# Attention's products in four visits for five, with the value sums in one gap

## The chip, the core and the metric

The kernel runs on one core of a Trainium2 chip. A core has TensorE for matmuls (PE in the profile; PEld is its weight load), VectorE (DVE), ScalarE (ACT), GpSimd (POOL) and SyncE (SP), which issues most of the transfers. Each engine works through its own instructions in order and waits on semaphores that the others raise. Matmuls write to PSUM, which has eight banks of 512 fp32 columns. The metric is the device time of one execution in microseconds.

## The reference

Four layers on x of 2048 tokens by 512 features, in the order A, B, A, B, each x + layer(layernorm(x)). There are 32 heads of 16 features. A is a linear attention with learned features and is not touched by the change. B cuts the tokens into four segments of 512. For each segment and head it computes

```python
logits = jnp.einsum("bhqd,bhkd->bhqk", qs, ks) * scale + mask   # causal, 512 x 512
p = _softmax(logits, axis=-1)
a_dot = jnp.einsum("bhqk,bhkd->bhqd", p, vs)
num = jnp.einsum("bhld,bhde->bhle", pq, M)                      # memory of earlier segments
den = jnp.einsum("bhld,bhd->bhl", pq, z)[..., None] + 1e-6
o = g * (num / den) + (1.0 - g) * a_dot
M = M + jnp.einsum("bhld,bhle->bhde", pk, vs)                   # pk = phi(ks)
z = z + jnp.einsum("bhld->bhd", pk)
```

and then o @ wo. Everything is fp32 in and out.

## The kernel before

A layer B is `LayerB.steps`. Four segments times four chunks of eight heads times two make 32 half chunks of four heads, numbered m = 0 to 31. The four heads of a half chunk are two for each half of the PE array: e = 0 uses rows 0 to 63, e = 1 rows 64 to 127, and r = 0, 1 counts the heads in each half. [...] The 512 queries and keys of a head are four blocks of 128.

Work comes in three kinds. `maxima` multiplies queries by keys into the banks mx (e = 0) and my (e = 1), and VectorE takes the row maximum of each product with the causal mask added (`tensor_tensor_reduce`, in the profile CUSTOM_DVE_ANT_0 and a read of the accumulator). `put_maxima` turns the sixteen columns of maxima with a transpose and sends them back, by a transfer from ScalarE's queue, as one more row of the queries, so that the logits come out reduced by their maximum. `attend` multiplies keys by queries (transposed logits) into lg, a tile of two banks, ScalarE takes the Exp into an SBUF tile of tag P4, and GpSimd sets the part above the diagonal to zero (`affine_select`). `weighted` multiplies these by the values, 16 matmuls on four column strips of the array, into the bank pv; ScalarE copies pv to U, and `finish` transposes U and lets VectorE divide by the sums (`weigh`), whose result GpSimd adds to the memory's part.

Time in `steps` is counted in gaps k, R = 5 to a half chunk. At the start of each gap stands a visit: one round of `attend` for the half chunk at hand (`next(at)`) and one of `maxima` for a later one (`next(ma)`, LEAD = 9 gaps ahead). The five rounds of `attend` are block 0 of r = 0, block 0 of r = 1, blocks 1 and 3 of r = 0, the same of r = 1, and block 2 of both. After the visit come steps that were put off (`late`: names that end in ~ in the tables, mostly VectorE's low part of a product that was split into a rounded high part and the rest), then, in gaps 0 and 2, half of `weighted` for the half chunk before, then `later` (the feature map of a projection, on ScalarE and GpSimd), and then what the tables FIRST, GAPS, LAST or FINAL list for that gap, such as a projection in quarters (q, k, v, out), `fin` for `finish`, `a` for the memory's product and its weighing, `t` and `m` for the update of the memory, `turn` for transposed rows, `ln` or `n` for a step of the layer norm. In gaps 0 and 2 the tables list nothing of size.

All of these, but for visits and value sums, take their PSUM tile from the tag g with G = 3 banks. So the eight banks are 3 g, 2 lg, mx, my, pv. Which of the three a tile gets is decided when the program is built; a matmul that opens a tile waits for the last reader of the bank's previous tile. VectorE's, ScalarE's and GpSimd's instructions keep the order in which they are written (`Ordered`), PE's too (`held`).

Layer A's second pass runs as side work in the first gaps of a layer B, and the next layer A's first pass in its last.

## Time and profile before

| | us |
|---|---|
| median of 3 runs | 1522.89 (1522.32 to 1524.72) |
| the profiled execution's own time | 1523.71 |
| its span, first to last instruction | 1521.9 |
| first layer B's half chunks | from 320.6 to about 768 |
| second layer B's half chunks | from 1064.9 to 1504 |

The profile was taken on one execution. A row of the timeline gives the start in us from the start of the span, the duration, the engine, the line, the operation, what it writes and reads (out<-in by tile names), the shape and how many such instructions follow one another; in brackets stands idle time before it and what ended it. Almost all rows have lines L163, L185 or L189, which are helpers, so tiles tell more than lines. A matmul's row is longer than the time to the next matmul's start, because matmuls overlap; the time between starts is what counts on PE.

### The profile page before, as it was taken

The page shows a single profiled execution, that of the slowest core. Times are in us where ns is not written, and L with a number is a line of the kernel's source. Part 1 is how long each engine was busy: PE and PEld are TensorE (multiplying, and loading weights), DVE is VectorE, ACT ScalarE, POOL GpSimd, SP SyncE. Part 2 cuts the span into 40 slices and gives each one's busy share as a digit, 9 for nine tenths or more (in the row PEclk, how much of TensorE's full clock was granted, in tenths as well). Part 3 has the DMA queues.
Part 4 walks back from the last instruction along what each step waited for, and adds up shares of the span by engine and source line. Part 5 has one row for each costly group of instructions (what it writes and reads, how often), then busy time and mean ns, then how long its engine had stood idle before and what let it go on. Part 6 is the DMA issues. An engine that isn't in the chain of part 4 may idle for free.

```text
span 1521.9 us, 30316 instructions
## 1 busy us (share of the span) xinstructions
PE 1456.3 (96%) x10888; PEld 1033.4 (68%) x10888; DVE 1095.3 (72%) x3258; ACT 787.1 (52%) x1178; POOL 650.3 (43%) x1000
## 2 busy tenths in 40 slices
PE   7999989999999999999999998999999999999998
PEld 6877767765666666666667786776656666666554
DVE  4765868668778877878656667757688788787783
ACT  5554335436565566556544333443565656655553
POOL 1668654313454544433314445541344445444331
PEclk9999999999999999999999999999999999999999
DMA  5487265545444443535340122744463353443340
GB/s 183 129 289 254 70 210 165 167 119 153 122 110 117 135 104 103 157 99 147 114 143 33 39 84 80 225 148 144 113 175 106 105 153 99 111 118 98 80 112 36
DMA packets 108773, 195.85 MB, mean 129 GB/s; under 512 B 14416, under 2 KB 27856, under 8 KB 107856
## 3 DMA queue, kind: packets, MB, share of 16 engines
q1 hardware_dynamic: 107472, 193.38, 42.8%
q8 instruction: 88, 1.44, 0.4%
q10 hardware_dynamic: 1152, 0.52, 0.1%
q14 instruction: 61, 0.50, 0.1%
HBM read 101.05 MB, written 39.85 MB: 93 GB/s over the span
## 4 chain that ended last, share of the span: by engine, by line
PE 78%; DVE 12%; ACT 4%; issue 2%; POOL 2%; DMA 1%; SPq 0%; ACTq 0%; POOLq 0%; DVEq 0%
PE g L185 45%; PE pv L185 9%; PE lg L185 9%; PE g L189 7%; PE mx L185 5%; PE my L185 3%; DVE mx L163 2%; POOL P L163 2%; DVE es L163 2%; ACT P L163 1%; DVE my L163 1%; DVE mxs L163 1%; ACT tb L163 1%; DVE hl L163 1%; DVE ol L163 1%
## 5 line engine op out<-in xcount | busy, mean ns | idle before, releaser
L163 ACT ACTIVATE P<-lg 128x1024 f32<-128x1024 f32 x320 | 328.9, 1028 | 173.0 <-PE lg L185 165.5
L163 POOL TENSOR_SCALAR_AFFINE_SELECT P<-P 128x256 f32<-128x256 f32 (+1 forms) x448 | 190.7, 440 | 442.3 <-ACT P L163 441.7
L163 DVE CUSTOM_DVE_ANT_0 mx<-mx,mask 128x128 f32<-128x128 f32 (+3 forms) x512 | 255.3, 499 | 160.7 <-PE my L185 109.0
L163 DVE CUSTOM_DVE_ANT_0 my<-my,mask 128x128 f32<-128x128 f32 (+3 forms) x512 | 265.9, 519 | 6.5
L185 PE MATMUL g<-hh,wqk 128*128 128x512 f32 x512 | 180.5, 407 | 2.1 <-ACT hh L163 1.4
L185 PE MATMUL lg<-e,e 64*128 64x256 f32 (+2 forms) x1024 | 168.4, 387 | 7.8 <-ACT P L163 7.6
L185 PE MATMUL g<-w,oh 128*128 128x512 f32 x512 | 170.6, 414 | 3.5 <-DVE ol L163 1.6
L185 PE MATMUL pv<-P,v 128*32 128x512 f32 (+3 forms) x2048 | 165.0, 441 | 0.0
L185 PE MATMUL my<-e,e 63*128 63x256 f32 (+2 forms) x512 | 146.7, 346 | 5.3 <-DVE mxs L163 3.9
L185 PEld LDWEIGHTS lg<-e,e 64*128 64x128 f32 x1024 | 81.1, 184 | 103.2 <-issue 50.6
L185 PE MATMUL g<-w,hh 128*128 128x512 f32 x448 | 145.8, 406 | 0.9 <-ACT tb L163 0.9
L163 DVE DVE_READ_ACCUMULATOR2_ANT mxs<- 128x1 f32 x1024 | 145.0, 142 | 0.0
L185 PE MATMUL mx<-e,e 63*128 63x256 f32 (+2 forms) x512 | 140.8, 330 | 0.2
L185 PEld LDWEIGHTS pv<-P,v 128*32 128x32 f32 x2048 | 53.7, 109 | 100.9 <-issue 92.0
L185 PEld LDWEIGHTS g<-hh,wqk 128*128 128x128 f32 x512 | 96.3, 188 | 24.0 <-ACT hh L163 1.8
L185 PEld LDWEIGHTS g<-w,oh 128*128 128x128 f32 x512 | 89.4, 190 | 30.9 <-issue 5.7
L185 PE MATMUL g<-w,ol 128*128 128x512 f32 x256 | 101.8, 398 | 0.0
L185 PE MATMUL g<-hl,wqk 128*128 128x512 f32 x256 | 100.4, 392 | 0.4 <-DVE hl L163 0.4
L163 POOL TENSOR_SCALAR tb<-tb 128x512 f32<-128x512 f32 x48 | 71.5, 1489 | 67.4 <-ACT tb L163 67.4
L163 ACT CAST ta<-g 128x512 fp32r<-128x512 f32 x64 | 37.6, 587 | 112.5 <-PE g L185 112.2
L185 PEld LDWEIGHTS my<-e,e 63*128 63x128 f32 x512 | 82.0, 185 | 18.1 <-DVE mxs L163 8.8
L185 PEld LDWEIGHTS mx<-e,e 63*128 63x128 f32 x512 | 89.7, 186 | 6.1 <-issue 3.6
(143 smaller groups left out, 2816.8 us busy)
## 6 DMA issues: line engine op xcount, KB each, us to landing
e<-ta SPq DMA_DIRECT2D x384, 128.0 KB
wqk<-wqk SPq DMA_DIRECT2D x64, 512.0 KB
x<-x SPq DMA_DIRECT2D x48, 256.0 KB
ot<-in SPq DMA_DIRECT2D x28, 256.0 KB
pq<-tb SPq DMA_DIRECT2D x24, 256.0 KB
tb<-pq SPq DMA_DIRECT2D x24, 256.0 KB
x<-xr SPq DMA_DIRECT2D x24, 256.0 KB
xr<-x SPq DMA_DIRECT2D x24, 256.0 KB
```

The source lines that it names most:

```text
L163: i = f(*a, **k)
L185: return held(nc.tensor.matmul(*a, **k))
L189: return held(nc.tensor.transpose(*a))
```

## The change

R goes from 5 to 4. `attend` has four rounds, one for each r and e: block 0 of one head of half e and blocks 1 and 3 of the head of the other half, in lg, then one Exp and two masks. The rounds with r = 1 have block 2 of both heads of half e too, in a bank of its own, mz, with an Exp of 512 columns and one mask. `maxima` also has four rounds; the first and the last hold two more products each, in mz. `attend` uses mz in gaps 2 and 3 and `maxima` in gaps 0 and 1. `weighted` runs once, in gap 0, with all 16 products; its tile comes from g, and the bank pv is gone (8 banks: 3 g, 2 lg, mx, my, mz). The tables are written anew for four gaps: what stood in gap 3 stands in gap 2, and what stood in gap 4 in gap 3; LEAD, FINAT, BEGIN, MAXIMA and BEFORE follow. The diff, cut (FIRST, LAST, FINAL and BEFORE change in the same manner as GAPS):

```diff
-PV = 1
 G = 3
-R = 5
-FILL = (1, 3, 4)
-LEAD = 9
-FINAT = 8
+R = 4
+LEAD = 7
+FINAT = 6
...
-BEGIN = -25
-MAXIMA = -9
+BEGIN = -22
+MAXIMA = -7
...
 GAPS = """
-0.2 n              | 0.3 a1 fin v3/3 n
-0.1 max a1 k2~     | 0.4 v3 turn~ m0
-1.0 n              | 1.2 n
-1.1 max q3~        | 1.3 fin out/2     | 1.4 out t1 turn~
-2.1 max a2 m1 k3~  | 2.3 fin ln out/3  | 2.4 out turn~ ln
-3.1 max ln ln out~ | 3.3 a2 fin q0+/2  | 3.4 q0+~ t2
-4.1 max k0+~ a3 turn~ load | 4.3 a3 fin out/3 | 4.4 out~ m2
-5.0 n              | 5.3 fin v0+/2 n N
-5.1 max q1+~ begin | 5.4 v0+ t3
-6.0 N              | 6.1 max a0+ k1+~  | 6.2 n
-6.3 a0+ fin v1+/3 N | 6.4 v1+ m3       | 7.0 n N
-7.1 max q2+~       | 7.2 n N           | 7.3 fin v2+/2 n N
-7.4 v2+ t0+
+0.2 a1 fin v3/3 n
+0.1 max a1 k2~ n   | 0.3 v3 turn~ m0
+1.0 n
+1.1 max q3~ n      | 1.2 fin out/2     | 1.3 out t1 turn~
+2.1 max a2 m1 k3~  | 2.2 fin ln out/3  | 2.3 out turn~ ln
+3.1 max ln ln out~ | 3.2 a2 fin q0+/2  | 3.3 q0+~ t2
+4.1 max k0+~ a3 turn~ load | 4.2 a3 fin out/3 | 4.3 out~ m2
+5.0 n              | 5.2 fin v0+/2 n N
+5.1 max q1+~ begin | 5.3 v0+ t3
+6.0 N              | 6.1 max a0+ k1+~ n
+6.2 a0+ fin v1+/3 N | 6.3 v1+ m3       | 7.0 n N
+7.1 max q2+~ n N   | 7.2 fin v2+/2 n N
+7.3 v2+ t0+
 """
...
-            for what in ([(0, 0, 0), (0, 2, P)], [(0, 3, 0)], [(1, 0, 0), (1, 2, P)],
-                         [(0, 1, 0), (1, 1, 256)], [(1, 3, 0)]):
+            for r, e, three in ((0, 1, True), (0, 0, False), (1, 1, False), (1, 0, True)):
                 pb = [PS(t, 1) for t in ("mx", "my")]
-                for r, i, at in what:
-                    prod(pb, r, i, at, max(256, (i + 1) * P))
-                for e in range(2):
-                    for r, i, at in what:
-                        top(pb, e, r, i, at)
+                parts = [(pb[1 - e], 1 - e, r, 0, 0), (pb[1 - e], 1 - e, r, 2, P), (pb[e], e, r, 3, 0)]
+                if three:
+                    pz = PS("mz", 1)
+                    parts.insert(0, (pz, e, 0, 1, 0))
+                    parts.insert(2, (pz, e, 1, 1, 256))
+                for part in parts:
+                    prod(*part)
+                if not three:
+                    parts = [parts[i] for i in (0, 2, 1)]
+                for part in parts:
+                    top(*part)
                 self.mx[m] = mx
                 yield
...
-            for kbs, r in (((0,), 0), ((0,), 1), ((1, 3), 0), ((1, 3), 1), ((2,), None)):
-                pb = PS("lg", 1, (P, 2, 512))
...
+            for r in range(2):
+                for e in range(2):
+                    f = 1 - e
+                    pb = PS("lg", 1, (P, 2, 512))
+                    pr = T2("P4", NP4, shape=(P, 2, 512))
...
+                    prod(pb[:, f, 256:512], f, r, 3, 256)
+                    prod(pb[:, e, :], e, r, 0, 512)
+                    prod(pb[:, f, 0:384], f, r, 1, 384)
+                    exp_of(pr, pb, pr[:, e : e + 1, 0:P], pr.rearrange("p e (b x) -> p e b x", b=4)[:, f, 0:4:3, :])
+                    if r > 0:
+                        pz = PS("mz", 1)
+                        if e == 0:
+                            p2 = T2("P4", NP4, shape=(P, 2, 512))
+                        for rr in range(2):
+                            prod(pz[:, 256 * rr : 256 * rr + 256], e, rr, 2, 256)
+                            self.pr[m][2, rr, e] = p2[:, e, 256 * rr : 256 * rr + 256]
+                        exp_of(p2[:, e, :], pz, p2[:, e, :].rearrange("p (r x) -> p r x", r=2)[:, :, 0:P])
+                    yield
...
-            if not last:
-                self.pv[m] = PS("pv", PV)
-            pv, pr = self.pv[m], self.pr[m]
-            for kb in ((1, 2) if last else (0, 3)):
+            pv, pr = PS("g", G), self.pr.pop(m)
+            for kb in (0, 3, 1, 2):
...
-            for k in range(BEGIN, R * N + 4):
+            for k in range(BEGIN, R * N + 1):
...
-                if k % R in (0, 2) and 0 <= k // R - 1 < N:
-                    self.weighted(k // R - 1, k % R == 2)
+                if k % R == 0 and 0 <= k // R - 1 < N:
+                    self.weighted(k // R - 1)
```

More of the change, by code (lines that the diff above doesn't have):

```diff
@@ L52 @@
 FIRST = """
-0.1 max k2/2       | 0.2 v3/2          | 0.3 k2~
-0.4 v3             | 1.1 max m0 q3/2   | 1.3 fin q3~       | 1.4 t1 k3/1
-2.1 max m1 k3      | 2.3 fin ln~       | 2.4 ln~ ln~
-3.3 fin q0+/2      | 3.0 w
-3.1 max ln~        | 3.4 q0+~ t2
-4.1 max k0+/2 load | 4.3 fin k0+/1     | 4.4 k0+ m2
-5.0 n              | 5.3 fin q1+/2 n
-5.1 max v0+        | 5.4 q1+~ t3
-6.1 max a0+ v1+    | 6.2 n             | 6.3 a0+ fin k1+/2
-6.4 k1+ m3         | 7.0 n             | 7.2 n
-7.1 max q2+~       | 7.3 fin v2+/2 n   | 7.4 v2+ t0+
+0.0 v3/2
@@ L64 @@
+0.1 max k2/2       | 0.2 k2~           | 0.3 v3
+1.1 max m0 q3/2    | 1.2 fin q3~       | 1.3 t1 k3/1
+2.1 max m1 k3      | 2.2 fin ln~       | 2.3 ln~ ln~
+3.2 fin q0+/2      | 3.0 w
+3.1 max ln~        | 3.3 q0+~ t2
+4.1 max k0+/2 load | 4.2 fin k0+/1     | 4.3 k0+ m2
+5.0 n              | 5.2 fin q1+/2 n
+5.1 max v0+        | 5.3 q1+~ t3
+6.1 max a0+ v1+ n  | 6.2 a0+ fin k1+/2
+6.3 k1+ m3         | 7.0 n
+7.1 max q2+~ n     | 7.2 fin v2+/2 n   | 7.3 v2+ t0+
 """
 GAPS = """
-0.2 n              | 0.3 a1 fin v3/3 n
@@ L79 @@
+7.3 v2+ t0+
 """
 LAST = """
-0.1 max a1 k2~     | 0.2 n             | 0.3 a1 fin v3/3 n
-1.0 n              | 0.4 v3 turn~      | 1.2 n
-1.1 max q3~        | 1.3 fin out/2     | 1.4 out turn~
-2.1 max k3~        | 2.3 fin a2 out/2  | 2.4 out a2 turn~
-3.1 max ln~ ln~    | 3.3 fin out/2 ln~ | 3.4 out ln~ turn~
-4.1 max v/2        | 4.3 fin out/2     | 4.4 out v
-5.1 max v/2        | 5.3 fin v         | 5.4 a3 pre
-6.1 max v/2        | 6.3 fin v a3      | 6.4 v/2 pt~
-7.1 p v pt~        | 7.3 fin v/2 p pt  | 7.4 v p pt
+0.1 max a1 k2~ n   | 0.2 a1 fin v3/3 n
@@ L91 @@
+1.0 n              | 0.3 v3 turn~
+1.1 max q3~ n      | 1.2 fin out/2     | 1.3 out turn~
+2.1 max k3~        | 2.2 fin a2 out/2  | 2.3 out a2 turn~
+3.1 max ln~ ln~    | 3.2 fin out/2 ln~ | 3.3 out ln~ turn~
+4.1 max v/2        | 4.2 fin out/2     | 4.3 out v
+5.1 max v/2        | 5.2 fin v         | 5.3 a3 pre
+6.1 max v/2        | 6.2 fin v a3      | 6.3 v/2 pt~
+7.1 p v pt~        | 7.2 fin v/2 p pt  | 7.3 v p pt
 """
 FINAL = """
-0.1 max k2~        | 0.3 fin v3/3      | 0.4 v3 a1
-1.1 max a1 q3/2    | 1.3 fin q3~       | 1.4 turn~
@@ L95 @@
-2.1 max k3/2       | 2.3 fin k3        | 2.4 out/2
-3.1 max a2 out turn~ | 3.3 fin out/2   | 3.4 out~ a2
-4.1 max a3 turn~   | 4.3 fin out/2     | 4.4 out/1 a3
-5.1 max out turn~  | 5.3 fin out/2     | 5.4 out/1 pre
-6.1 max out~       | 6.3 fin           | 6.4 pt~
-7.1 p pt~          | 7.3 fin p pt      | 7.4 p pt
-"""
-BEFORE = {-25: "q0 load", -23: "v0", -21: "k0",
-          -18: "n", -17: "v1 n", -16: "n", -15: "n n", -14: "q1 n", -13: "n", -12: "k1 n", -11: "n", -10: "v2 n",
-          -4: "max q2~", -1: "t0"}
+0.1 max k2~        | 0.2 fin v3/3      | 0.3 v3 a1
@@ new lines @@
+1.1 max a1 q3/2    | 1.2 fin q3~       | 1.3 turn~
+2.1 max k3/2       | 2.2 fin k3        | 2.3 out/2
+3.1 max a2 out turn~ | 3.2 fin out/2   | 3.3 out~ a2
+4.1 max a3 turn~   | 4.2 fin out/2     | 4.3 out/1 a3
+5.1 max out turn~  | 5.2 fin out/2     | 5.3 out/1 pre
+6.1 max out~       | 6.2 fin           | 6.3 pt~
+7.1 p pt~          | 7.2 fin p pt      | 7.3 p pt
+"""
+BEFORE = {-22: "q0 load", -20: "v0", -18: "k0",
+          -15: "n", -14: "v1 n", -13: "n", -12: "n n", -11: "q1 n", -10: "n", -9: "k1 n", -8: "n", -7: "v2 n",
+          -3: "max q2~", -1: "t0"}
@@ L906, in __init__ @@
             self.st, self.hT, self.vv, self.ot, self.mx, self.U = {}, {}, {}, {}, {}, {}
-            self.pr, self.pv = {}, {}
+            self.pr = {}
             self.later, self.late, self.rows, self.turned = [], [], [], []
@@ L1023, in maxima, with prod @@
             mx = T2("mxs", 2, shape=(P, 16))
-            def prod(pb, r, i, at, w):
-                for e in range(2):
-                    q, k = Q[64 * e : 64 * e + 63, r, :], K[64 * e : 64 * e + 63, r, :]
-                    mm(pb[e][:, at : at + w], lhsT=q[:, i * P : (i + 1) * P], rhs=k[:, 0:w],
-                       start=True, stop=True, tile_position=(64 * e, 0))
+            def prod(pb, e, r, i, at):
+                w = max(256, (i + 1) * P)
+                q, k = Q[64 * e : 64 * e + 63, r, :], K[64 * e : 64 * e + 63, r, :]
+                mm(pb[:, at : at + w], lhsT=q[:, i * P : (i + 1) * P], rhs=k[:, 0:w],
+                   start=True, stop=True, tile_position=(64 * e, 0))
             def top(pb, e, r, i, at):
@@ L1033, in top @@
                 col = (e * 2 + r) * 4 + i
-                pl = pb[e][:, at : at + n]
+                pl = pb[:, at : at + n]
                 with tc.high_priority():
@@ L1038, in top @@
                         op0=ADD, op1=MAX, accum_out=mx[:, col : col + 1])
-            for what in ([(0, 0, 0), (0, 2, P)], [(0, 3, 0)], [(1, 0, 0), (1, 2, P)],
-                         [(0, 1, 0), (1, 1, 256)], [(1, 3, 0)]):
+            for r, e, three in ((0, 1, True), (0, 0, False), (1, 1, False), (1, 0, True)):
                 pb = [PS(t, 1) for t in ("mx", "my")]
-                for r, i, at in what:
-                    prod(pb, r, i, at, max(256, (i + 1) * P))
-                for e in range(2):
-                    for r, i, at in what:
-                        top(pb, e, r, i, at)
+                parts = [(pb[1 - e], 1 - e, r, 0, 0), (pb[1 - e], 1 - e, r, 2, P), (pb[e], e, r, 3, 0)]
[9 more added lines that the diff above has]
+                    top(*part)
                 self.mx[m] = mx
@@ L1065, in attend, with prod, exp_of @@
             self.pr[m] = {}
-            def prod(pb, r, kb, at, w):
-                for e in range(2):
-                    q, k = Q[64 * e : 64 * e + 64, r, :], K[64 * e : 64 * e + 64, r, :]
-                    mm(pb[:, e, at : at + w], lhsT=k[:, kb * P : (kb + 1) * P],
-                       rhs=q[:, 512 - w : 512], start=True, stop=True, tile_position=(64 * e, 0))
-            for kbs, r in (((0,), 0), ((0,), 1), ((1, 3), 0), ((1, 3), 1), ((2,), None)):
-                pb = PS("lg", 1, (P, 2, 512))
-                pr = T2("P4", NP4, shape=(P, 2, 512))
-                pq = pr.rearrange("p e (b x) -> p e b x", b=4)
-                if kbs == (0,):
-                    prod(pb, r, 0, 0, 512)
-                    diags = [pr[:, :, 0:P]]
-                elif kbs == (1, 3):
-                    prod(pb, r, 3, 256, 256)
-                    prod(pb, r, 1, 0, 384)
-                    diags = [pq[:, e, 0:4:3, :] for e in range(2)]
-                else:
-                    for rr in range(2):
-                        prod(pb, rr, 2, 256 * rr, 256)
-                    diags = [pr.rearrange("p e (r x) -> p (e r) x", r=2)[:, :, 0:P]]
-                self.pr[m][kbs, r] = pr
+            def prod(out, e, r, kb, w):
+                q, k = Q[64 * e : 64 * e + 64, r, :], K[64 * e : 64 * e + 64, r, :]
+                mm(out, lhsT=k[:, kb * P : (kb + 1) * P],
+                   rhs=q[:, 512 - w : 512], start=True, stop=True, tile_position=(64 * e, 0))
+            def exp_of(pr, pb, *diags):
                 with tc.high_priority():
@@ L1092, in attend, with weighted @@
                     pool.affine_select(out=diag, in_=diag, pattern=[[0, diag.shape[1]], [1, P]],
-                                            compare_op=ALU.is_ge, fill=0.0, base=0, channel_multiplier=-1)
-                yield
-        def weighted(self, m, last):
+                                       compare_op=ALU.is_ge, fill=0.0, base=0, channel_multiplier=-1)
+            for r in range(2):
[3 more added lines that the diff above has]
+                    pr = T2("P4", NP4, shape=(P, 2, 512))
+                    self.pr[m][0, r, e] = pr[:, e, :]
+                    self.pr[m][1, r, f] = pr[:, f, 0:384]
+                    self.pr[m][3, r, f] = pr[:, f, 384:512]
+                    prod(pb[:, f, 256:512], f, r, 3, 256)
[11 more added lines that the diff above has]
+                    yield
+        def weighted(self, m):
             s, c, hf = m // 8, m % 8 // 2, m % 2
             v = self.vv[s][0]
-            if not last:
-                self.pv[m] = PS("pv", PV)
-            pv, pr = self.pv[m], self.pr[m]
-            for kb in ((1, 2) if last else (0, 3)):
+            pv, pr = PS("g", G), self.pr.pop(m)
+            for kb in (0, 3, 1, 2):
                 for r in range(2):
@@ L1107, in weighted @@
                         h = c * 8 + hf * 4 + hh
-                        if kb == 0:
-                            p = pr[(0,), r][:, e, :]
-                        elif kb == 2:
-                            p = pr[(2,), None][:, e, 256 * r : 256 * r + 256]
-                        else:
-                            p = pr[(1, 3), r][:, e, 0:384] if kb == 1 else pr[(1, 3), r][:, e, 384:512]
                         mm(pv[32 * hh : 32 * hh + 32, kb * P : 512],
-                           lhsT=v[:, kb, h * VW : h * VW + 32], rhs=p,
+                           lhsT=v[:, kb, h * VW : h * VW + 32], rhs=pr[kb, r, e],
                            start=(kb == 0), stop=(kb == 2), tile_position=(0, 32 * hh))
-            if last:
-                self.pr.pop(m)
-                U = T2("U", 2)
-                act.activation(U, self.pv.pop(m), AF.Identity, scale=share[:, m % 8 : m % 8 + 1])
-                self.U[m] = U
+            U = self.U[m] = T2("U", 2)
+            act.activation(U, pv, AF.Identity, scale=share[:, m % 8 : m % 8 + 1])
         def finish(self, m):
```

## The prediction

> **What bounds the kernel now.** I read the page first, for the engine that carries the span and for the chain of waits.

> ```profile
> span 1521.9 us, 30316 instructions
> PE 1456.3 (96%) x10888; PEld 1033.4 (68%) x10888; DVE 1095.3 (72%) x3258; ACT 787.1 (52%) x1178; POOL 650.3 (43%) x1000
> PE 78%; DVE 12%; ACT 4%; issue 2%; POOL 2%; DMA 1%; SPq 0%; ACTq 0%; POOLq 0%; DVEq 0%
> ```

> PE is busy for 96% of the span and holds 78% of the chain. Then I cut the two attention stages into stretches (busy time by stretch: PE, PEld, DVE, ACT, POOL); the first row is the second segment of the first layer B, eight half chunks, the second the sum over both stages.

> ```profile
> 429.72:546.87 117.15, 116.57 (x857) 78.58 (x856) 92.24 (x329) 71.07 (x103) 54.74 (x95) 1.00 0.43 119
> sum 874.06, PE 856.92 PEld 560.98 DVE 673.34 ACT 512.16 POOL 366.48; mean PE 107.11 PEld 70.12 DVE 84.17 ACT 64.02 POOL 45.81
> ```

> In the middle segments PE is idle for 0.6 us of 117, and in both stages together for 17 of 874. So whatever the change saves must be saved in PE's own work, and any new wait of PE is added in full. Third, PE's timeline through one half chunk:

> ```profile
> 429.72 0.50 PE L185 MATMUL lg<-e,e 64*128 64x512 f32 x2
> ...
> 430.39 1.28 PE L185 MATMUL pv<-P,v 128*32 128x512 f32 x16
> 431.60 0.50 PE L185 MATMUL lg<-e,e 64*128 64x512 f32 x2
> ...
> 432.44 0.28 PE L189 MATMUL g<-ident,mxs 128*16 128x128 f32 x1
> 432.55 0.63 PE L185 MATMUL g<-mem,tb 128*128 128x136 f32 x4
> ...
> 435.86 0.56 PE L185 MATMUL lg<-e,e 64*128 64x256 f32 x4
> ...
> 436.58 1.28 PE L185 MATMUL pv<-P,v 128*32 128x384 f32 x16
> 437.80 0.56 PE L185 MATMUL lg<-e,e 64*128 64x256 f32 x4
> ...
> 438.64 0.73 PE L185 MATMUL g<-mem,tb 128*128 128x136 f32 x4
> 439.21 0.60 PE L189 MATMUL g<-ident,U 128*128 128x128 f32 x4
> 439.81 0.73 PE L185 MATMUL g<-w,hh 128*128 128x512 f32 x2
> ```

> Each visit starts at an lg row and ends at the next row that is neither lg, mx nor my. The first lasts 0.67 us (512 logit and 512 maxima columns in each half of the array, 1024), the second 0.84 (1152), the third 0.72 (1152), the fourth 0.84 (1280). The fifth has 1024 columns like the first; I take 0.67. Together 3.74 us. Behind the first and the third come the value sums, 1.21 and 1.22 us. Fourth, VectorE's timeline across the third and fourth visits:

> ```profile
> 436.69 0.70 DVE L163 CUSTOM_DVE_ANT_0 mx<-mx,mask 128x512 f32<-128x512 f32 x1 [1.55 <-PE my L185]
> 437.30 0.14 DVE L163 DVE_READ_ACCUMULATOR2_ANT mxs<- 128x1 f32 x1
> ...
> 437.95 0.69 DVE L163 TENSOR_TENSOR ta<-g,ta 128x512 fp32r<-128x512 f32 x1
> 438.68 0.30 DVE L163 CUSTOM_DVE_ANT_0 mx<-mx,mask 128x128 f32<-128x128 f32 x1
> ...
> 439.07 0.57 DVE L163 CUSTOM_DVE_ANT_0 mx<-mx,mask 128x384 f32<-128x384 f32 x1
> 439.55 0.14 DVE L163 DVE_READ_ACCUMULATOR2_ANT mxs<- 128x1 f32 x1
> ...
> 440.46 0.17 DVE L163 TENSOR_SCALAR r<-g 128x16 f32<-128x16 f32 x1
> 440.67 0.25 DVE L163 RECIPROCAL r<-r 128x16 f32<-128x16 f32 x1
> 440.95 0.42 DVE L163 TENSOR_TENSOR ot<-g,r 128x256 f32<-128x256 f32 x1
> ```

> It gives the step from one maximum to the next: 0.61 us for 512 columns, 0.39 for 128, 0.48 for 384. More important is what happens to the g banks. The projection that ended at 435.8 gives up its bank when VectorE has taken the low part (437.95 to 438.64). PE has no use for that bank before 439.81, because the 1.22 us of value sums and the fourth visit lie between. The value gap of today is time in which VectorE catches up.

> **The change, part by part.** (Half chunks: 32 in each of two layers, 64.)

> Visits. The same matmuls come in four visits. From the order of the built program, the fuller half of the array has 1536 columns in every visit (512 + 1024), the other 1280. From 0.67 (1024) to 0.72 (1152) a further 128 columns cost 0.05, from 0.67 to 0.84 (1280) 0.085; four times that more gives 0.87 to 1.01 us a visit. The second and fourth visit hold a short wait for VectorE, so I stay near the lower end: 0.90, four make 3.60 against 3.74. Saved 0.14 x 64, 9 us; bounds 17 us saved to 19 us lost (3.48 and 4.04).

> Value sums. The same 16 products, one time instead of two. What goes is one way into and one out of that layout of the array. A visit of 1024 columns at 0.05 per 128 would be 0.40, so 0.27 of its 0.67 us is fixed; a value gap's fixed part is between nothing and that. I take 0.13: 64 x 0.13, 8 us saved, bounds 0 and 17.

> [...]

> Idle PE. Of the 17 us some are short waits in visits and at segment ends; a third bank for maxima and fewer, longer gaps may end a few: 3 us saved, bounds 0 and 10.

> ScalarE and GpSimd. ScalarE has four Exps of 1024 columns and two of 512 for five of 1024, GpSimd ten masks for seven, with the same columns in all.

> ```profile
> L163 ACT ACTIVATE P<-lg 128x1024 f32<-128x1024 f32 x320 | 328.9, 1028 | 173.0 <-PE lg L185 165.5
> L163 POOL TENSOR_SCALAR_AFFINE_SELECT P<-P 128x256 f32<-128x256 f32 (+1 forms) x448 | 190.7, 440 | 442.3 <-ACT P L163 441.7
> ```

> ScalarE sat 173 us idle ahead of these Exps and GpSimd 442 us ahead of the masks; even with each of the three added masks at a full 0.44 us that is 84 us of GpSimd work. I cost both at nothing, covered by PE's work in the gaps. Where that cover is thin: the value sums now need the masks of the visit just before. Its Exp starts some 0.7 us into that visit, ends at 1.7, its masks by about 2.7; the value sums start one gap and one visit later, 3.4 us or more after it. That leaves 0.7 us, unless GpSimd is at other work (rival below).

> VectorE. The same 16 maxima per half chunk, but 5, 3, 3, 5 to a visit. Behind the two visits of five lie the value gap and a whole projection (2.8 us or more), which cover them.

> The g banks. This is the term that decides. The value sums now take one of the three g banks, and the gap of the third visit follows directly on that of the second. I compared, in both built programs, which VectorE instruction each matmul's semaphore waits for. Before the change no matmul of a middle segment waits for a VectorE instruction that stands behind the maxima of its own visit. After it, such waits are in 26 gaps, 13 in each layer, all behind the third visit: where that gap needs three banks (memory or transposed rows, `finish`, and a projection), the third is free only after VectorE has worked through the new maxima, then the low part that was put off to here, then more.

> VectorE's side, from the start of the third visit: today the first maximum starts 0.83 after it (435.86 to 436.69) with 1152 columns; now the two products in my end after 1280 columns and one turn of waiting for their place in PE's order, so 0.95. Maxima 0.39 + 0.61 + 0.48 make 2.43, the low part 0.69 makes 3.12. A further low part makes 3.8; a weighing of two steps (0.28 + 0.42) also 3.8; one of three (0.21 + 0.28 + 0.42) 4.0. PE's side: visit 0.90, memory product 0.57 (438.64 to 439.21), four transposes at 0.11 (432.44 to 432.55), so it wants the third bank at 1.9.

> Four gaps (half chunks 8 and 16 of a layer, a value projection behind the weighing of its own memory product) wait 2.1 to 2.2 us; four (10 and 18, an output projection behind `finish`'s weighing) 2.0; four (11 and 19, a query projection behind the residual's add) 1.3. These make 22 us. The other 14 wait for a low part or for one and a further, and want their bank at 1.4 to 1.9: 1.0 to 2.4 each, together 23 us; the three in the last half chunks count 1.0, as little other work is left there. Sum 45 us. Bounds: 26 x 0.7 = 18 if VectorE is half a microsecond earlier and PE as much later, 26 x 2.2 = 57 if all are of the longest kind. I stay at the worked 45.

> End of a stage. The last value sums wait for Exp and masks of the last visit, where today half of them need older ones: 1 us for each layer, 2.

> Sum: 1523.7 (the profiled execution: span 1521.9, and 1.8 around it) - 9 - 8 - 3 + 45 + 2 = 1550.7. The median of the runs, 1522.9, lies 0.8 below that execution, so 1550.

> **Rivals.** *The bank waits don't bite* (faster). All savings come, 20 us: 1503; with the whole fixed part of 0.27 us saved twice in each half chunk it would be 35 us, 1488. It decides at 20 / 26, 0.77 us per gap: below that the change wins. For it: PE could reach the third bank later than 1.9, if visits are longer than 0.90. Against it: VectorE's order is fixed, and its chain to 3.1 is made of rows alone but for the first 0.95. Chance 0.14.

> *They cancel* (no change): waits of about 0.8 us each, 1523. Chance 0.06.

> *The value sums wait for their masks* (slower still). In gaps where GpSimd has the two 512-column steps of a feature map,

> ```profile
> L163 POOL TENSOR_SCALAR tb<-tb 128x512 f32<-128x512 f32 x48 | 71.5, 1489 | 67.4 <-ACT tb L163 67.4
> ```

> masks queue behind 1.5 us and as much again. At 0.5 us on average it adds 32 us: 1582. For it: GpSimd's queue is in order. Against it: these steps mostly land behind the third visit, early enough. Chance 0.12.

> *The halves don't run side by side* (much slower). Matmuls of the two halves now come in uneven turns. In series, 2816 columns at 0.05 per 128 make 1.37 a visit with its fixed part, 0.47 more, 120 us: about 1670. Against it: the uneven starts of the second visit today still overlap. Chance 0.03.

> **How the numbers follow.** My own case has the rest, 0.65, with its own range 1532 to 1570 from the bounds of the bank term. Slower by over 0.2%: 0.65 + 0.12 + 0.03 = 0.80; within 0.2% (3 us, about what a measurement of this kernel can tell from no change) 0.06; faster 0.14. The range 1510 to 1580 takes in mine, the cancelled case, the slower end up to where masks cost 0.5 us, and the upper part of the faster case; it leaves out some 0.17.

> **What would show it.** Visits of 0.90 us, four to a half chunk, and one value gap of about 2.3 us would show the savings. In half chunks 8 and 16, PE should stand still 2 us ahead of the value projection in the third gap, released by VectorE's `ot`; the list of waits should have entries of PE g on VectorE's ot, wt, ta, ol and xr that today's middle segments lack, some 45 us in all; PE's idle time in the stages should go from 17 to about 60 us. I am wrong if that list stays short, if a value gap starts behind GpSimd, or if a visit takes over a microsecond.

## The result, and the profile after

The changed kernel takes 1557.5 us (median of 6 runs, 1553.7 to 1563.5) where the kernel before takes 1523.4 us on the same chip (6 runs, 1522.1 to 1524.9): 1.0225 times as long, 95% interval 1.0202 to 1.0248. The forecast was 1550, range 1510 to 1580. The profiled execution of the changed kernel is its shortest, 1553.74 us.

The page of the changed kernel (span; busy time by engine; the chain's shares):

```profile
span 1552.0 us, 30551 instructions
PE 1451.1 (93%) x10888; PEld 1054.5 (68%) x10888; DVE 1055.7 (68%) x3258; ACT 776.9 (50%) x1242; POOL 675.4 (44%) x1192
PE 76%; DVE 12%; ACT 5%; POOL 3%; issue 3%; DMA 1%; SPq 0%; ACTq 0%; DVEq 0%; POOLq 0%
```

The two attention stages cut into their segments of eight half chunks, changed kernel (length; busy PE, PEld, DVE, ACT, POOL; granted clock; DMA share; GB/s). The two rows are the second segments of the two layers B, the sum is over all eight segments:

```profile
427.87:555.38 127.51, 118.36 (x857) 82.61 (x856) 87.28 (x329) 69.33 (x112) 57.78 (x119) 0.97 0.40 109
...
1187.41:1315.20 127.79, 118.29 (x857) 82.59 (x856) 87.27 (x329) 69.47 (x112) 57.81 (x119) 0.97 0.40 109
...
sum 918.31, PE 868.70 PEld 593.48 DVE 642.30 ACT 507.75 POOL 393.74; mean PE 108.59 PEld 74.19 DVE 80.29 ACT 63.47 POOL 49.22
```

The same cut through the kernel before:

```profile
sum 887.94, PE 870.49 PEld 570.00 DVE 679.57 ACT 518.74 POOL 369.54; mean PE 108.81 PEld 71.25 DVE 84.95 ACT 64.84 POOL 46.19
```

The stages are 30.4 us longer, which is the whole loss of the profiled execution (1553.74 - 1523.71 = 30.0). PE is busy for as long as before, and idle for 49.6 us instead of 17.5. A second segment, 117.15 us before, takes 127.5, and PE stands still in it for 9.15 us where it was 0.6. Its granted clock is 0.97 where it was 1.00; that column turns out to matter.

PE and VectorE together across the third visit and the third gap of half chunk 16 (first layer B, changed kernel):

```profile
563.71 0.56 PE L185 MATMUL lg<-e,e 64*128 64x256 f32 x3
...
564.60 0.30 DVE L163 CUSTOM_DVE_ANT_0 my<-my,mask 128x128 f32<-128x128 f32 x1 [1.38 <-PE my L185]
564.61 0.73 PE L185 MATMUL g<-mem,tb 128*128 128x136 f32 x4
...
564.82 0.73 DVE L163 CUSTOM_DVE_ANT_0 mx<-mx,mask 128x512 f32<-128x512 f32 x1
565.18 0.60 PE L189 MATMUL g<-ident,U 128*128 128x128 f32 x4
...
565.46 0.60 DVE L163 CUSTOM_DVE_ANT_0 my<-my,mask 128x384 f32<-128x384 f32 x1
...
565.98 0.69 DVE L163 TENSOR_TENSOR ta<-g,ta 128x512 fp32r<-128x512 f32 x1
566.58 0.17 DVE L163 TENSOR_SCALAR r<-g 128x16 f32<-128x16 f32 x1
...
567.07 0.42 DVE L163 TENSOR_TENSOR ot<-g,r 128x256 f32<-128x256 f32 x1
...
567.64 0.70 PE L185 MATMUL g<-w,hh 128*128 128x512 f32 x2 [1.86 <-DVE ot L163]
```

The visit lasts 0.90 us (563.71 to 564.61). PE has done the memory product and the transposes at 565.78 and then stands still for 1.86 us: the value projection wants the third bank, and VectorE works through three maxima, the low part `ta` put off to here, and `r` and `ot` of the memory product before it gives that bank back. The list of PE's waits over the two middle segments of the first layer, complete, changed kernel (us in total, times, longest):

```profile
PE g L185 <- DVE ot L163: 3.7, 2, 1.9
PE g L185 <- DVE wt L163: 3.6, 2, 1.8
PE g L185 <- DVE r L163: 2.1, 2, 1.0
PE g L189 <- DVE r L163: 2.1, 1, 2.1
PE g L185 <- ACT tb L163: 2.1, 1, 2.1
PE g L189 <- DVE ta L163: 1.4, 1, 1.4
PE g L185 <- DVE ta L163: 0.9, 1, 0.9
PE g L185 <- ACT v L163: 0.8, 2, 0.6
```

That is 16.7 us. The same list of the kernel before, whole, has 1.0 us:

```profile
PE g L185 <- ACT v L163: 0.5, 2, 0.3
PE my L185 <- DVE mxs L163: 0.5, 2, 0.3
```

Over the whole span, PE's waits for a g bank on VectorE add up to 58.6 us instead of 16.2. Behind the third visits alone, PE's waits for a g bank are 41 us, in 14 gaps of each layer; in the kernel before, behind the fourth visits, where the same cells stand, they are 0.8 us.

The value sums show a second loss. Sixteen of the 64 last 2.42 to 3.51 us where the others last about 2.29, 11 us in all. (The very last one of the second layer is left out: its weights wait for no mask, and PE then waits 0.81 us for ScalarE, as it does in the kernel before.) The one of half chunk 16 of the second layer, all engines, changed kernel:

```profile
1312.39 1.09 ACT L163 ACTIVATE tb<-g 128x512 f32<-128x512 f32 x2 [0.88 <-DVE ta L163]
1313.08 1.49 POOL L163 TENSOR_SCALAR tb<-tb 128x512 f32<-128x512 f32 x1 [0.97 <-ACT tb L163]
...
1314.65 1.27 POOL L163 TENSOR_TENSOR tb<-tb,tb 128x512 f32<-128x512 f32 x1
...
1315.88 0.73 POOL L163 TENSOR_TENSOR tmp<-tmp,wt 128x256 f32<-128x256 f32 x1
...
1316.56 0.66 POOL L163 TENSOR_SCALAR_AFFINE_SELECT P<-P 128x128 f32<-128x128 f32 x2
1316.91 0.19 PEld L185 LDWEIGHTS g<-P,v 128*32 128x32 f32 x6 [0.66 <-POOL P L163]
```

The value sums' weights wait 0.66 us for GpSimd's masks. These stand in its queue behind the two steps of a feature map (and, in this half chunk, behind one addition, `tmp`), which started late because ScalarE's Exp had waited 0.88 us for VectorE's low part `ta`: the same put-off low part as above, at the other end of a chain.

A third loss is in the clock. Two stretches of 3.41 us of the changed kernel, the one that holds the standstill of half chunk 8 and the next:

```profile
437.26:440.67 3.41, 1.56 (x9) 1.15 (x8) 2.54 (x10) 2.14 (x4) 2.44 (x4) 1.00 0.54 186
440.67:444.08 3.41, 3.41 (x14) 2.13 (x12) 0.17 (x1) 0.70 (x1) 1.28 (x1) 0.50 0.00 0
```

PE stands still for 1.85 us of the first, and in the second its clock is 0.50. PE does about half the work per us there: two projection matmuls take 0.85 us (441.03 to 441.88) where two like them took 0.45 just before (440.19 to 440.64). Such half-clock time is 38 us in this execution and 17 us in that of before; at half the work per us that is an estimated 19.1 and 8.7 us lost.

### The profile page after: what moved, and what is told of

It reads as the page before. It is cut to its first block, busy times and chain, and to the rows that moved or that the text cites. A ratio compares the mean times of both kernels' runs of the same rounds, so it can differ in the third digit from the quotient of the medians.

```text
span 1552.0 us, 30551 instructions
## 1 busy us (share of the span) xinstructions
PE 1451.1 (93%) x10888; PEld 1054.5 (68%) x10888; DVE 1055.7 (68%) x3258; ACT 776.9 (50%) x1242; POOL 675.4 (44%) x1192
## 3 DMA queue, kind: packets, MB, share of 16 engines
q10 hardware_dynamic: 1152, 0.52, 0.1%
## 4 chain that ended last, share of the span: by engine, by line
PE 76%; DVE 12%; ACT 5%; POOL 3%; issue 3%; DMA 1%; SPq 0%; ACTq 0%; DVEq 0%; POOLq 0%
PE g L185 54%; PE lg L185 8%; PE g L189 7%; PE my L185 3%; PE mx L185 3%; DVE my L163 2%; PE mz L185 2%; ACT P L163 2%; DVE es L163 2%; ACT tb L163 1%; POOL P L163 1%; DVE mx L163 1%; DVE ol L163 1%; DVE ta L163 1%; DVE mxs L163 1%
## 5 line engine op out<-in xcount | busy, mean ns | idle before, releaser
L163 POOL TENSOR_SCALAR_AFFINE_SELECT P<-P 128x256 f32<-128x256 f32 (+1 forms) x640 | 214.6, 363 | 438.6 <-ACT P L163 438.2
L163 ACT ACTIVATE P<-lg 128x1024 f32<-128x1024 f32 x256 | 263.2, 1028 | 146.2 <-PE lg L185 133.1
L163 DVE CUSTOM_DVE_ANT_0 my<-my,mask 128x512 f32<-128x512 f32 (+2 forms) x384 | 210.9, 549 | 76.8 <-PE my L185 76.6
L163 DVE CUSTOM_DVE_ANT_0 mx<-mx,mask 128x128 f32<-128x128 f32 (+2 forms) x384 | 210.8, 549 | 73.5 <-PE mx L185 71.9
L185 PE MATMUL g<-hh,wqk 128*128 128x512 f32 x512 | 182.5, 411 | 6.9 <-DVE r L163 4.2
L185 PE MATMUL g<-w,oh 128*128 128x512 f32 x512 | 172.2, 418 | 11.6 <-DVE wt L163 7.2
L163 DVE CUSTOM_DVE_ANT_0 mz<-mz,mask 128x256 f32<-128x256 f32 x256 | 114.9, 449 | 79.3 <-PE mz L185 41.4
L185 PE MATMUL g<-P,v 128*32 128x512 f32 (+3 forms) x2048 | 161.3, 436 | 1.2 <-DVE tb L163 0.6
L185 PE MATMUL g<-w,hh 128*128 128x512 f32 x448 | 147.7, 411 | 15.4 <-DVE ot L163 7.4
L185 PE MATMUL lg<-e,e 64*128 64x256 f32 (+2 forms) x768 | 144.6, 409 | 1.8 <-ACT P L163 1.4
L163 DVE DVE_READ_ACCUMULATOR2_ANT mxs<- 128x1 f32 x1024 | 145.9, 142 | 0.0
L185 PEld LDWEIGHTS lg<-e,e 64*128 64x128 f32 x768 | 76.6, 187 | 84.9 <-issue 69.5
L185 PEld LDWEIGHTS g<-P,v 128*32 128x32 f32 x2048 | 65.8, 109 | 81.5 <-issue 63.6
L185 PEld LDWEIGHTS g<-hh,wqk 128*128 128x128 f32 x512 | 97.7, 191 | 32.0 <-ACT P L163 5.0
L185 PEld LDWEIGHTS g<-w,oh 128*128 128x128 f32 x512 | 90.4, 192 | 41.4 <-issue 21.9
L185 PE MATMUL my<-e,e 63*128 63x512 f32 (+2 forms) x384 | 111.7, 344 | 2.3 <-DVE mxs L163 1.7
L185 PE MATMUL mx<-e,e 63*128 63x256 f32 (+2 forms) x384 | 112.4, 346 | 0.0
L185 PEld LDWEIGHTS g<-w,hh 128*128 128x128 f32 x448 | 80.0, 191 | 38.4 <-issue 14.1
L185 PE MATMUL g<-w,ol 128*128 128x512 f32 x256 | 103.0, 402 | 3.3 <-DVE ol L163 3.3
L163 POOL TENSOR_SCALAR tb<-tb 128x512 f32<-128x512 f32 x48 | 71.5, 1490 | 78.5 <-ACT tb L163 78.5
L185 PE MATMUL mz<-e,e 63*128 63x256 f32 (+1 forms) x512 | 105.2, 285 | 0.0
L185 PE MATMUL g<-hl,wqk 128*128 128x512 f32 x256 | 101.9, 398 | 3.1 <-DVE hl L163 3.1
```

The lines of the kernel that those rows point to most:

```text
L163: i = f(*a, **k)
L185: return held(nc.tensor.matmul(*a, **k))
```

## The experiments

All stand beside runs of the kernel before on the same chip (1522.5 and 1522.6 us). The table shows the profiled executions. PE's timeline is divided into visits, value sums and the rest, each piece lasting from its first weight load to the first of the next piece; some work on the same tiles outside the stages, the same in all, is contained. "Lost to the clock" is an estimate, half of the time at half clock.

| kernel | time | visits | value sums | rest | lost to the clock |
|---|---|---|---|---|---|
| before | 1523.7 | 399.9 | 197.9 | 903.6 | 8.7 |
| changed | 1553.7 | 380.4 | 195.4 | 955.0 | 19.1 |
| changed, projection first | 1523.1 | 378.7 | 194.6 | 926.9 | 10.8 |
| changed, low parts at once | 1502.1 | 378.0 | 187.3 | 913.9 | 7.0 |
| changed, both edits | 1489.3 | 378.2 | 186.2 | 901.1 | 6.5 |
| changed, no min and add | 1553.5 | 380.8 | 186.0 | 963.4 | 25.5 |
| changed, stalls filled | 1547.4 | 379.0 | 195.6 | 950.6 | 10.6 |
| before, sums together | 1582.1 | 464.9 | 186.1 | 908.4 | 16.2 |
| before, both edits | 1542.6 | 424.1 | 197.2 | 899.8 | 5.0 |

### Projection first in the third gap

```diff
-0.2 a1 fin v3/3 n
+0.2 v3/3 a1 fin n
...
-2.2 fin ln out/3
+2.2 out/3 fin ln
...
-3.2 a2 fin q0+/2
+3.2 q0+/2 a2 fin
...
-6.2 a0+ fin v1+/3 N
+6.2 v1+/3 a0+ fin N
```

(only the changed cells are shown; 0.2, 2.2 and 3.2 of the last segment change in the same way)

> The changed kernel (1557.5 us), with one edit: in the third gap of a half chunk the projection is written ahead of the memory product, the transposed rows and `finish` (six cells of the tables: chunk halves 0, 2, 3, 6 of the middle segments, 2 and 3 of the last). It then takes a bank that is free, and what waits for VectorE's weighing is moved behind it. Theory A (the waits for the third bank decide, some 40 us): the waits of 2 us ahead of value and output projections and of 1.2 us ahead of the query projection go, about 10 gaps in each layer, 25 to 30 us in all; what comes third in the gap now waits for less, 0 to 0.5 us. Time 1525 to 1540. Theory B (the value sums' waits for their masks are what costs): nothing changes, 1552 to 1560. Theory C (the granted clock fell because of something else than the stalls, and that is what costs): 1550 to 1560, with the same number of stretches at half clock, ten.

Measured: 1525.1 us, 1.0013 times the kernel before (1.0004 to 1.0023). The list of PE's waits over the same two segments falls from 16.7 to 6.7 us; its first rows:

```profile
PE g L189 <- ACT tb L163: 2.2, 5, 0.4
PE g L189 <- DVE r L163: 2.1, 1, 2.1
```

The entries for `ot` and `wt` are gone. No engine has more or less to do: the order within six cells is worth 32 us, the upper end of what theory A gave, and 8 of it is the clock's (19.1 to 10.8). The value sums stay as slow as they were (194.6), so the masks were not what this edit mended.

### Low parts at once

```diff
-0.1 max a1 k2~ n   | 0.3 v3 turn~ m0
+0.1 max a1 k2 n    | 0.3 v3 turn~ m0
...
-7.1 max q2+~ n N   | 7.2 fin v2+/2 n N
+7.1 max q2+ n N    | 7.2 fin v2+/2 n N
```

(and so in all cells of the second gap, in all four tables; `turn~`, `ln~` and `pt~` there lose their ~ too)

> The changed kernel with the other edit: the low parts of the projections in the second gap are taken at once instead of behind the next visit (all ~ in the tables' second-gap cells dropped); the order in the third gap stays. VectorE then has only the maxima to do behind the third visit before the third bank is free, 2.4 us after that visit's start (0.95 + 0.39 + 0.61 + 0.48) where PE wants it at 1.9. Theory A (waits for the third bank decide): of about 40 us of waits 25 to 40 go; the low parts end no later than before the third visit's maxima, so that nothing new waits: 1518 to 1535. Rival D (the low parts at once hold up the third visit's maxima, and the fourth visit waits for banks of maxima): the waits move to mx and my, 0.3 to 0.7 us in 64 half chunks, and the time stays at 1545 to 1570. Theory B: 1552 to 1560.

Measured: 1502.0 us, 0.9863 (0.9847 to 0.9880), well below what I expected. The same list over the two segments, whole:

```profile
PE g L185 <- ACT tb L163: 6.0, 6, 1.1
PE g L185 <- ACT v L163: 1.1, 2, 0.6
PE g L185 <- DVE tmp L163: 0.5, 1, 0.5
```

Every wait for VectorE's `ot`, `wt`, `r` and `ta` is gone; what is left waits for ScalarE, but for 0.5 us. Rival D falls: the visits don't get longer (378.0). What I had not counted is that the value sums recover as well, from 195.4 to 187.3, though GpSimd has all its steps: with the low part early, ScalarE's Exp and GpSimd's two steps start early too.

### Both edits

> The changed kernel with both edits together. Theory A: no third bank is waited for; PE idle in the two attention stages falls from 50 us to about 20, what is left being the value sums' waits for masks (11 us): 1510 to 1522, so at or under the kernel before. If the clock's stretches at half speed came with the stalls, they fall from ten to five or six again. Theory B or C: 1545 to 1560.

Measured: 1490.0 us (1486.3 to 1494.2), 0.9786 (0.9765 to 0.9807): faster than both kernels, 67 us below the changed one. The second segments, the sum over all eight, and the whole list of waits over the two middle segments of the first layer:

```profile
425.03:539.79 114.76, 113.18 (x857) 80.22 (x856) 87.37 (x329) 69.04 (x111) 57.47 (x118) 1.00 0.45 121
...
sum 856.27, PE 846.57 PEld 587.54 DVE 644.00 ACT 510.64 POOL 392.80; mean PE 105.82 PEld 73.44 DVE 80.50 ACT 63.83 POOL 49.10
```

```profile
PE g L185 <- ACT v L163: 0.9, 2, 0.6
PE g L185 <- DVE tmp L163: 0.5, 1, 0.5
PE g L185 <- ACT tb L163: 0.5, 1, 0.5
```

1.9 us instead of 16.7. The sum runs 4 us past the last visit of the first layer, where the ones above end with that visit, so it is its idle time that compares: 9.7 us, where it was 49.6 in the changed kernel and 17.5 in the kernel before. The clock is 1.00 again in every segment. The value sums of half chunk 16 in the second layer, all engines, as above for the changed kernel:

```profile
1264.61 1.49 POOL L163 TENSOR_SCALAR tb<-tb 128x512 f32<-128x512 f32 x1
...
1268.10 1.03 POOL L163 TENSOR_SCALAR_AFFINE_SELECT P<-P 128x128 f32<-128x128 f32 x3
...
1268.62 2.36 PE L185 MATMUL g<-P,v 128*32 128x512 f32 x32
```

GpSimd starts the feature map's first step 4.0 us before the value sums, where it was 3.0 (1313.08 and 1316.10), so the masks are done in time. Against the kernel before, visits are 21.7 us shorter, value sums 11.7 and the rest 2.5, together 35.9; the profiled executions differ by 34.4.

### Without GpSimd's two steps

```diff
-                    pool.tensor_scalar(e, e, 1.0, None, op0=MIN)
-                    pool.tensor_tensor(out=e, in0=e, in1=r, op=ADD)
```

> The changed kernel without GpSimd's two steps of the feature map (the minimum with 1 and the addition of the relu part are left out, so the memory reads and writes use other features). GpSimd's queue then holds almost nothing but masks. In the profile of the changed kernel 16 of 64 value sums last 2.42 to 3.56 us where the others last 2.29, an excess of 11 us in all. Theory B (these wait for masks that queue behind those steps): the excess goes to under 2 us, and the time falls by 8 to 12 us, to 1545 to 1549. Theory A: the waits for the third bank stay at about 40 us, so the time does not fall by more than that. If the value sums wait for something else: 1555 to 1560.

Measured: 1548.6 us (1546.4 to 1553.5), 1.0175 (1.0153 to 1.0196), 9 us below the changed kernel, as theory B's part of the expectation had it. The value sums fall by 9.4 us, to 186.0, so it was those steps that held the masks; the list of PE's waits for banks stays at 16.7 us, row for row. The profiled execution is the longest of its runs: in it the clock takes back 6.4 us (25.5 for 19.1), which is why the table shows no gain for it.

### The stalls filled with work

```diff
-            for t in range(4):
+            for t in [0, 1, 2, 3] * (3 if m in (7, 9, 13, 15, 17) else 1):
                 tp(pt[:, t * P : (t + 1) * P], U[:, t * P : (t + 1) * P], ident)
...
-                    for q in range(2):
+                    for q in [0, 1] * (3 if a and (s, c) == (1, 3) else 1):
                         mm(pn[:, q * 8 * VW : (q + 1) * 8 * VW],
```

> The changed kernel (1557.5 us) with more work for TensorE and nothing else: in the gaps of half chunks 8, 10, 14, 16 and 18 of a layer the four transposes of `finish` are done three times over into the same bank (8 more, 0.9 us), and in half chunk 12 the memory product's two (three times over, 1.2 us). They stand where TensorE waits 1.4 to 2.1 us for the third bank, so the waits get shorter by what is added. Theory C (TensorE standing still for over half of a stretch of 3.41 us brings the next stretch at half clock): of the ten half-clock stretches in the profile of the changed kernel the five that follow those gaps go, each worth 1.7 us: 1546 to 1551, although TensorE does about 11 us more. If the half clock has nothing to do with the stalls: as many such stretches, 1556 to 1560. If the added work lies on the path: 1562 to 1570.

Measured: 1549.4 us (1547.4 to 1552.7), 1.0179 (1.0162 to 1.0196): 8 us faster than the changed kernel, with more to do. One window of 127 us, first this kernel, then the changed one:

```profile
426.00:553.00 127.00, 121.07 (x907) 85.19 (x907) 88.08 (x334) 71.37 (x114) 59.70 (x122) 1.00 0.42 112
```

```profile
426.00:553.00 127.00, 117.85 (x854) 82.35 (x856) 86.89 (x329) 68.82 (x110) 57.54 (x118) 0.97 0.40 109
```

The clock is back at 1.00 there, and at 0.994 over the span (0.988 in the changed kernel). All five half-clock stretches that followed the long waits are gone and others remain, an estimated 8.5 us less lost. This is most of the clock's part of the loss (10.4 us, 19.1 against 8.7), measured by itself.

### The value sums together, in the kernel before

```diff
-                if k % R in (0, 2) and 0 <= k // R - 1 < N:
-                    self.weighted(k // R - 1, k % R == 2)
+                if k % R == 0 and 0 <= k // R - 1 < N:
+                    self.weighted(k // R - 1, False)
+                    self.weighted(k // R - 1, True)
```

> The kernel before (1522.6 us) with one part of the change alone: all 16 value sums stand behind the first of the five visits, in their own bank; behind the third visit there is no gap, so that the fourth follows directly on it. Savings alone: one way into and out of the sums' layout less, 64 x 0.13 = 8 us, and up to 17: 1506 to 1515. My reading that the second value gap was time in which VectorE and ScalarE catch up: the fourth visit now waits for the Exp of the third to empty the bank of logits (1.03 us that start some 0.65 after the third visit's first product, so about 1 us where PE wants to go on after 0.72) and for the third's maxima; 1 to 1.5 us in 64 half chunks, 60 to 95 us, so 1575 to 1610.

Measured: 1583.9 us, 1.0398 (1.0377 to 1.0419). The first row of the list of PE's waits over the whole span:

```profile
PE lg L185 <- ACT P L163: 63.4, 73, 2.2
```

0.87 us each time, where the kernel before has 7.6 us of it in all. The value sums themselves gain 11.8 us (197.9 to 186.1), between my estimate of 8 and its bound of 17. So the second value gap was cover, as I had read it, but for ScalarE's Exp more than for VectorE (PE's waits for a g bank on VectorE stay at 16.2 us): merging the sums alone loses 61 us, and here it became a gain together with visits rearranged so that a whole gap follows each.

### Both edits in the kernel before

The same reordering and the same ~ dropped in the tables of the kernel before.

> The kernel before (1522.6 us) with the two edits of the combination that runs in 1490 us: projection first in the gap behind the fourth visit, low parts of the second gap taken at once. Theory A (the edits only undo waits that the change brought; the five visits with two value gaps leave no bank waited for): within 5 us of the kernel before, 1517 to 1527. Rival E (the edits are good by themselves, and the change has no part in the gain): 1490 to 1505.

Measured: 1541.7 us, 1.0121 (1.0105 to 1.0136). Both theories missed: the edits make the kernel before 19 us slower. PE and VectorE across its third and fourth visits, half chunk 8:

```profile
436.20 0.69 DVE L163 TENSOR_TENSOR ta<-g,ta 128x512 fp32r<-128x512 f32 x1 [1.47 <-ACT ta L163]
436.81 0.69 DVE L163 CUSTOM_DVE_ANT_0 mx<-mx,mask 128x512 f32<-128x512 f32 x1
...
437.41 0.56 PE L185 MATMUL lg<-e,e 64*128 64x256 f32 x4
...
437.42 0.73 DVE L163 CUSTOM_DVE_ANT_0 my<-my,mask 128x512 f32<-128x512 f32 x1
...
438.26 0.38 PE L185 MATMUL my<-e,e 63*128 63x256 f32 x1 [0.17 <-DVE mxs L163]
```

The low part now stands ahead of the third visit's maxima. The second of them gives its bank back only 0.65 us after the fourth visit has begun (438.06 and 437.41), and the fourth visit waits for it; in the kernel before it was done 0.15 us after (437.80 and 437.95, in the rows shown with the prediction). Its median goes from 0.88 to 1.33 us, and the 64 fourth visits add up to 75.6 us instead of 55.8: 19.8 us, as much as the whole loss. (The first visits add another 4.8, and the pieces outside the visits give about as much back.) As these rows have it, the ~ protected the maxima behind a value gap that was too short to wait out a low part. The change took that gap away, and with it the reason for the ~, but left the ~ in place. The two edits were not tried one at a time in this kernel; that the dropped ~ costs and not the order is read from the rows.

## Why the prediction was right, and where it was off

- **The bank waits, +45 us**: right in place and mechanism, 42.4 us measured (58.6 - 16.2), and 41 us behind the third visits alone, in 28 gaps (26 forecast). In half chunks 8 and 16 PE stands 1.85 and 1.86 us (forecast 2.1 to 2.2), in 10 and 18 it is 1.80 (2.0), in 11 and 19 it is 1.03 and 1.04 (1.3; the list names `r`, not `xr`). VectorE's chain came 0.1 to 0.2 us sooner than worked out: its first maximum starts 0.89 behind the visit's start (0.95), the maxima end 2.27 behind it (2.43). Of the other waits the longest, 2.07 and 2.06 in half chunks 12 and 14, lie in the range given. Undoing these waits alone, without an instruction less, gives 32 us (projection first) and, with what hangs on them, 67 us (both edits).
- **Visits, -9 us**: the visit is the 0.90 us that was forecast (the halves run side by side in it: the first two logit products of the visit at 563.71, one on each half, start within 0.01 us), but the term was too small: -19.5. I took 3.74 us a half chunk from the one on show. Over all 64 the medians add up to 3.78 and the means to 4.00: before, the visits held waits of some 0.2 us that no row of mine showed. The second term, idle PE at -3, was meant for those and was too small.
- **Value sums, -8 us**: the gap is the 2.29 us that was forecast, but 16 wait for their masks, and -2.5 is left. This is the rival "the value sums wait for their masks", in part: 11 us instead of 32, where I had said that those steps land early enough. That is the step that failed; they are late because the put-off low part holds the Exp ahead of them. With it mended, merging brought 11.7 us.
- **The rest** agrees: PE's idle time in the stages went from 17 to 50 us (60 forecast). The 2 us forecast for the two stage ends did not come as described: the last value sums wait 0.55 us in the first layer, for VectorE's `tb`, and not at all in the second. VectorE's maxima and ScalarE's added instructions cost nothing that a row shows.
- **Missing from the sum: the clock.** An estimated 10 us of the 30 by which the profiled executions differ are PE at half clock. That the forecast came within 7 us of the median is in part luck: the clock's 10 us and the 5.5 us that the value sums did not gain were in good part made up by visits that gained 10 more than forecast.
- **The rival "the bank waits don't bite"** named 1503 and, with the whole fixed parts, 1488: with the waits taken away the kernel runs in 1490. The fixed part of 0.27 us is not shown right in size by that: at the medians four visits save 0.18 us a half chunk (3.78 to 3.60, 11.5 us in 64), and much of the rest are waits that went.

## What to carry to other kernels

When a change removes a gap, ask of every postponement in the code which gap it was postponed for: dropping the ~ (with the reorder) cost 19 us in the kernel before and gained 55 us by itself after the change. A buffer that is waited for can be mended by order as well as by number, with the work for which a buffer is already free written first. And count the waits of the engine that bounds over all repetitions, since the one on show is often the tidy one.

## What the runs showed of the hardware

```profile
563.55:566.96 3.41, 2.23 (x18) 1.58 (x16) 2.33 (x9) 2.26 (x4) 1.02 (x3) 1.00 0.62 190
566.96:570.37 3.41, 2.73 (x15) 2.09 (x17) 1.09 (x4) 1.52 (x3) 2.90 (x3) 1.00 0.13 48
```

These are two steps of the changed kernel; the standstill (1.86 us, 565.78 to 567.64) straddles them, PE is idle for 0.35 and 0.20 of them, and the clock stays at 1.00. The same standstill in the kernel without GpSimd's two steps:

```profile
564.19:567.60 3.41, 1.61 (x15) 1.12 (x11) 2.90 (x11) 2.53 (x5) 1.01 (x3) 1.00 0.75 233
567.60:571.01 3.41, 3.34 (x8) 2.70 (x9) 0.51 (x2) 0.91 (x2) 0.73 (x1) 0.50 0.00 0
```

It lies in one step (idle for 0.53 of it), and the next runs at 0.50. What decides among the 13 steps between 0.46 and 0.53, and in the one at 0.34, stays open. The spread of the run times goes with the clock: of the changed kernel's runs, 1553.7 to 1563.5 us, the two shortest have a mean granted clock of 0.988 and 0.991, the longest 0.984.
